# Attention of batch 0 in two query parts, with the first feed-forward matmuls beside the second part

## Chip, cores and metric

The kernel runs on one core of one Trainium2 chip. The metric is device time in microseconds (us) of that core. A "ratio" is the mean time of one kernel's runs over that of the other's runs of the same rounds, so it is not quite the ratio of the medians that are quoted.

Engines: PE is TensorE (matmul), ACT is ScalarE, DVE is VectorE, POOL is GpSimd, SP issues DMAs.

## The reference, cut to what matters

```python
# q, k, v: (8 batches, 12 heads, 448 tokens, 64); fp32
scores = q @ k.T / 8
attn   = maximum(scores, 0) ** 2 / 448
x      = (attn @ v), heads side by side          # 3584 tokens x 768
h      = maximum(x @ w_in, 0) ** 2               # w_in 768 x 2048
out    = h @ w_out                               # w_out 2048 x 768
```

## The kernel before

Heads go four at a time: a "unit" n is a third of a batch (24 units). A unit's score tile for key chunk t (64 keys) is 128 x 896; it is squared and masked on ACT and DVE ("soft"), and multiplied with v ("av"). The seven av steps of a unit sum into two PSUM tiles, which are copied to xt. When a batch's three units are done, its h groups (16 groups of 6 matmuls, each then squared into a tile g) and then its o groups (output) can run. Two stages follow from this. In the *stream*, batch 0's attention has nothing to hide behind. In the *dense stage*, PE works through a queue of h and o matmuls of one batch, and bursts of two score tiles of the next batch are put between them.

```python
def relu2(ps, dst, scale):                       # ACT Square, then DVE: (ps > 0) * dst
    nc.scalar.activation(out=dst, in_=ps, func=AF.Square, scale=scale)
    nc.vector.scalar_tensor_tensor(out=dst, in0=ps, scalar=0.0, in1=dst,
                                   op0=ALU.is_gt, op1=ALU.mult)
def relu2_wide(ps, dst, scale, eng):             # ACT Relu, then r*r on DVE or POOL
    ...
# the stream (batch 0 and two rounds of unit 3: 23 rounds)
for r in range(STREAM):
    n, t = divmod(r, TJ)
    sp = scores(n, t)                            # PE, 4 matmuls of 64x64 tiles, 448 columns
    soft(n, t, sp)                               # odd t: relu2_wide
    for z in late.get(r, (r - LAG,) if LAG <= r else ()):
        av(*divmod(z, TJ))                       # three rounds behind
    for fn, *a in beside.get(r, ()):             # casts, transposes, weight loads
        fn(*a)
push_dense(0)                                    # 16 h groups of 448 columns, then 6 o groups
for i in range(STREAM // 2, NB):                 # the dense stage
    ...                                          # two score tiles, av of a whole unit now and then
    run_some(max(0.0, (queued - KEEP) / (nxt - i)))
```

Score tiles live in two PSUM buffers (`sps`), everything else PE writes in four (`mmps`). PE, like SP, issues in the order in which the program is written. POOL issues the loads that change type (v and the weights), and casts q and k.

## Time and profile before

412.84 us (2 runs, 412.78 to 412.9); span 411.3 us.

| what | value | read from |
|---|---|---|
| stream, first score matmul to dense start | 7.84 to 37.86 us: 23 rounds, and the dense stage's first score tile at 37.34 us | timeline of PE |
| PE busy from 37.86 us to the end | 368.5 of 373.4 us; the rest is the last copy and store | table of stretches |
| PE waits in the stream | 9.7 us for score tiles to come free | waits |
| 128x896 eviction | ACT 0.92, DVE 1.09 us | groups |
| first 15 h matmuls | 5.24 us at half clock; later 3.00 us | timeline of PE |

The table of stretches of the kernel before (stretch in us, its length, then busy us and instructions of PE, PE's weight loads, DVE, ACT and POOL, then granted PE clock, DMA share and GB/s):

```profile
30.00:35.00 5.00, 2.74 (x32) 1.38 (x32) 4.14 (x4) 4.32 (x7) 0.74 (x1) 0.72 1.14 278
35.00:40.00 5.00, 4.32 (x26) 1.52 (x22) 3.61 (x5) 3.58 (x6) 0.67 (x1) 0.50 1.19 251
40.00:45.00 5.00, 5.00 (x36) 2.50 (x35) 2.81 (x5) 2.56 (x4) 1.19 (x3) 0.76 1.25 204
45.00:50.00 5.00, 5.00 (x33) 2.31 (x31) 4.69 (x7) 4.54 (x8) 4.61 (x7) 1.00 1.16 210
```

PE is full from 40 us on, but the clock is half until about 42 us. The whole dense stage in the same view:

```profile
37.86:411.27 373.41, 368.54 (x2860) 188.03 (x2856) 225.91 (x276) 233.72 (x376) 51.63 (x64) 0.99 0.55 116
```

The waits of the kernel before on PE, from 5 to 40 us (engine and line, for whom: us in total, times, longest):

```profile
PE sp L252 <- DVE at L155: 5.3, 4, 1.6
PE sp L252 <- ACT rel L161: 4.4, 4, 1.6
```

Both releasers free a score tile. No wait of PE is listed after the stream. The timeline of PE around the dense start (start us, us, instructions):

```profile
37.86 5.24 PE L176 MATMUL hps<-xt,w 128*128 128x448 f16 x15
...
44.33 3.00 PE L176 MATMUL hps<-xt,w 128*128 128x448 f16 x15
```

The same fifteen matmuls take 5.24 us, then 3.00 us.

### The profile page before, as it was taken

Reading aid. Unit: us, or ns where it says so; the run is one execution under the profiler, and the core shown is the slowest. Engines: PE = TensorE matmul, PEld = TensorE weight load, DVE = VectorE, ACT = ScalarE, POOL = GpSimd, SP = SyncE. Lnnn points to the kernel's source line nnn. Section 1 sums busy time; section 2 is a strip of 40 time slices with the busy share of each in tenths; the row PEclk is TensorE's granted clock in tenths of the full one; section 3 lists DMA queues with packets and bytes.
Section 4 is the critical chain, followed back from the end, with each engine's and each line's share of the span. In section 5 each row is a group of like instructions: output and inputs, shape, how many; then the busy total and the mean of one; then the engine's idle time right before and its main releaser. Section 6 shows DMA issues by size and latency. Waiting matters only on the chain.

```text
span 411.3 us, 7560 instructions
## 1 busy us (share of the span) xinstructions
PE 394.0 (96%) x3104; PEld 199.7 (49%) x3104; DVE 252.8 (61%) x304; ACT 259.7 (63%) x407; POOL 74.0 (18%) x95
## 2 busy tenths in 40 slices
PE   6847999999999999999999999999999999999995
PEld 2423455544455545544554544544554545555562
DVE  3987787578875777576655786576665686042200
ACT  3787787678866677666756767666756766333211
POOL 6861612123202301210302301210100000000000
PEclk9695999999999999999999999999999999999999
DMA  8999999599419750972829741881515010201132
GB/s 251 295 278 257 207 193 225 157 208 201 119 38 183 193 141 35 155 168 56 209 54 174 225 102 73 147 176 43 131 40 119 4 40 0 69 12 38 38 79 77
DMA packets 62914, 53.57 MB, mean 130 GB/s; under 512 B 35744, under 2 KB 59296, under 8 KB 62880
## 3 DMA queue, kind: packets, MB, share of 16 engines
q1 hardware_dynamic: 50672, 40.84, 40.7%
q0 software_dynamic: 11936, 11.80, 18.0%
q8 instruction: 24, 0.39, 0.4%
q10 hardware_dynamic: 272, 0.46, 0.3%
q14 instruction: 10, 0.08, 0.1%
HBM read 45.61 MB, written 11.01 MB: 138 GB/s over the span
## 4 chain that ended last, share of the span: by engine, by line
PE 91%; ACT 4%; DVE 2%; DMA 1%; issue 1%
PE hps L176 37%; PE ops L204 36%; PE sp L252 10%; PE avt L282 7%; ACT at L154 2%; ACT rel L161 1%; DMA kf<-in_k_dram 1%; DVE at L155 1%; PE tps L101 1%; ACT qT L103 0%; ACT xt L290 0%; DVE at L162 0%; DVE ks L87 0%; DVE kT L103 0%; DVE qT L103 0%
## 5 line engine op out<-in xcount | busy, mean ns | idle before, releaser
L155 DVE SCALAR_TENSOR_TENSOR at<-sp,at 128x896 f16<-128x896 f32 x159 | 166.3, 1085 | 82.1 <-ACT at L154 81.7
L154 ACT ACTIVATE at<-sp 128x896 f16<-128x896 f32 x159 | 137.7, 915 | 70.4 <-PE sp L252 70.4
L176 PE MATMUL hps<-xt,w 128*128 128x448 f16 x768 | 157.5, 356 | 0.0
L204 PE MATMUL ops<-w,g 128*128 128x384 f16 x896 | 156.8, 326 | 0.0
L204 PEld LDWEIGHTS <-g 128*128 128x128 f16 x896 | 84.4, 98 | 67.9 <-issue 13.7
L176 PEld LDWEIGHTS <-w 128*128 128x128 f16 x768 | 73.1, 99 | 75.1 <-issue 13.5
L155 DVE SCALAR_TENSOR_TENSOR g<-hps,g 128x448 f16<-128x448 f32 x128 | 75.7, 617 | 42.3 <-ACT g L154 42.0
L154 ACT ACTIVATE g<-hps 128x448 f16<-128x448 f32 x128 | 67.7, 551 | 29.7 <-PE hps L176 29.1
L252 PE MATMUL sp<-qT,kT 64*64 64x448 f16 x672 | 53.0, 373 | 10.6 <-DVE at L155 5.3
L211 ACT ACTIVATE osb<-ops 128x384 f32<-128x384 f32 x56 | 27.8, 496 | 37.8 <-PE ops L204 32.9
L87 POOL CAST ks<-kf 128x896 f16<-128x896 f32 x23 | 21.5, 935 | 147.6 <-DMA kf<-in_k_dram 109.8
L282 PE MATMUL avt<-at,vs 64*64 64x448 f16 x672 | 43.2, 363 | 0.4 <-ACT qT L103 0.3
L252 PEld LDWEIGHTS <-kT 64*64 64x64 f16 x672 | 16.5, 106 | 42.4 <-issue 39.7
L282 PEld LDWEIGHTS <-vs 64*64 64x64 f16 x672 | 21.5, 109 | 12.5 <-issue 2.7
L118 POOL DMA_DIRECT2D vs<-in_v_dram x28 | 17.4, 629 | 49.1 <-PE avt L282 48.3
L290 ACT ACTIVATE xt<-avt 128x448 f16<-128x448 f32 x48 | 23.6, 553 | 2.6 <-PE avt L282 2.5
L87 POOL CAST qs<-qf 128x896 f16<-128x896 f32 x23 | 23.2, 1009 | 6.7 <-DMA qf<-in_q_dram 6.7
L162 DVE TENSOR_TENSOR at<-rel 128x896 f16<-128x896 f32 x8 | 10.1, 1258 | 0.7 <-ACT rel L161 0.6
L161 ACT ACTIVATE rel<-sp 128x896 f32<-128x896 f32 x9 | 8.3, 922 | 2.2 <-PE sp L252 2.2
L345 PE MATMUL warm<-idle 128*128 128x512 f16 x12 | 4.6, 560 | 1.2 <-DVE idle L337 1.2
L129 POOL DMA_DIRECT2D w<-in_moe_w_out_dram x4 | 3.1, 764 | 14.2 <-DMA w<-in_moe_w_in_dram 14.2
L103 ACT COPY qT<-tps 128x896 f16<-128x896 f16 x5 | 4.5, 907 | 0.2 <-PE tps L101 0.2
(20 smaller groups left out, 31.4 us busy)
## 6 DMA issues: line engine op xcount, KB each, us to landing
kf<-in_k_dram SPq DMA_DIRECT2D x24, 448.0 KB, 5.1
out_dram<-osb SPq DMA_DIRECT2D x56, 192.0 KB, 2.7
qf<-in_q_dram SPq DMA_DIRECT2D x23, 448.0 KB, 5.7
vs<-in_v_dram POOLq DMA_DIRECT2D x28, 168.0 KB, 5.6
w<-in_moe_w_in_dram POOLq DMA_DIRECT2D x4, 768.0 KB, 22.2
w<-in_moe_w_out_dram POOLq DMA_DIRECT2D x4, 768.0 KB, 21.4
vs<-in_v_dram POOLq DMA_DIRECT2D x6, 112.0 KB, 7.9
qf<-in_q_dram ACTq DMA_DIRECT2D x1, 448.0 KB, 4.8
```

The costliest lines, as they stand in the source:

```text
L87: op(t.rearrange("p t (f d) -> p f t d", f=2), src.rearrange("p f (t d) -> p f t d", d=D))
L118: nc.gpsimd.dma_start(out=vst[b][rows, :, i], in_=src[:, :, h])
L154: nc.scalar.activation(out=dst, in_=ps, func=AF.Square, scale=scale)
L155: nc.vector.scalar_tensor_tensor(out=dst, in0=ps, scalar=0.0, in1=dst, op0=ALU.is_gt, op1=ALU.mult)
L161: nc.scalar.activation(out=r, in_=ps, func=AF.Relu, scale=scale)
L162: eng.tensor_mul(dst, r, r)
L176: nc.tensor.matmul(cell[0][:, 0:S], lhsT=w1[f // 4][:, m, (f % 4) * P:(f % 4 + 1) * P], rhs=xt[:, m, :], start=(m == 0), stop=(m == NM - 1))
L204: nc.tensor.matmul(cell[0][:, 0:HALF], lhsT=gt[f][:, tb * P:(tb + 1) * P], rhs=w2[f // 4][:, f % 4, hf * HALF:(hf + 1) * HALF], start=(f = ...
L211: nc.scalar.activation(out=cell[1][:, hf * HALF:(hf + 1) * HALF], in_=cell[0][:, 0:HALF], func=AF.Copy, scale=CO)
L252: nc.tensor.matmul(sp[64 * c:64 * c + 64, e, 0:S].rearrange("p (t c) -> p t c", t=TJ), lhsT=kT[r, t, 64 * e:64 * e + 64], rhs=qT[r, :, 64 ...
L282: nc.tensor.matmul(ap[f][64 * e:64 * e + 64, 0:S], lhsT=vs[r, u, e ^ c, t * D:(t + 1) * D], rhs=at[r, e, :], start=(t == 0), stop=(t == TJ ...
L290: nc.scalar.activation(out=xts[b][:, 2 * u + f, :], in_=ap[f][:, 0:S], func=AF.Copy, scale=CX)
```

## The change

The intent: batch 0's queries run as two parts, tokens 0 to 255, then 256 to 447. When the first part's attention is done, its columns of h can be computed beside the attention of the second part, where PE had idle time. Two key chunks share one score tile (2 x 256 = 512 or 2 x 192 = 384 columns). To have bandwidth for w_in in time, the loads of q and k for units 3 and 4 are put behind a "gate": a one-element memset in POOL's queue that the load must wait for. The first half of w_out's columns is loaded first. The diff, cut to its core:

```diff
-    def load_qk(n, w, eng):
+    def load_qk(n, w, eng, gate=None):
         ...
+        if gate is not None:
+            gate.memset(t[0:1, 0, 0:1], 0.0)
-    STREAM = NU * TJ + 2
+    STREAM = NU * TJ
+    PARTS = slice(0, 4 * TP), slice(4 * TP, S)
...
+        tiles = [(part, rounds[r:r + 2]) for part in range(2) for r in range(0, STREAM, 2)]
+        NA = len(tiles) // 2                                   # 11
+        engs = {1: nc.vector, 3: nc.vector, 5: nc.gpsimd, 7: nc.gpsimd, 9: nc.vector}
+        engs.update({NA + z: nc.gpsimd for z in (1, 3, 5, 7)})  # squares on POOL
+        engs[NA + 9] = nc.vector
         beside = {
...
+            NA + 1: [(load_w2, 0, 0), (load_w2, 0, 1),
+                     (load_qk, 3, "k", nc.sync, nc.gpsimd), (load_qk, 3, "q", nc.sync, nc.gpsimd)],
+            NA + 4: [(load_v, 1, slice(None))],
+            NA + 6: [(cast_qk, 3, "k", pool), (cast_qk, 3, "q", pool)],
+            NA + 7: [(load_qk, 4, "k", nc.sync, nc.gpsimd), (load_qk, 4, "q", nc.sync, nc.gpsimd)],
+            NA + 8: [(turn_pe, 3, "k", dve)],
+            NA + 9: [(turn_pe, 3, "q", act), (load_w2, 1, 0), (load_w2, 1, 1)],
         }
+        for i, (part, rs) in enumerate(tiles):
+            ...                                # scores of two chunks, soft
+            if i >= 2:
+                put(i - 2)                     # av, two tiles behind; part two's xt copies on DVE
+            if i > NA + 1:
+                for _, fn in h_group(0, done_h, PARTS[0]):
+                    fn()                       # one h group of 256 columns a tile, 11 in all
+                done_h += 1
...
-        hs = h_groups(b)
+        hs = h_groups(b) if b else (
+            [h_group(0, f, PARTS[0]) for f in range(done_h, NF)]
+            + [h_group(0, f, PARTS[1]) for f in range(NF)])
```

More of the change, by code (lines that the diff above doesn't have):

```diff
@@ L54 @@
     qkt_p = ctx.enter_context(tc.tile_pool(name="qktp", bufs=3))
-    at_p = ctx.enter_context(tc.tile_pool(name="atp", bufs=14))
+    at_p = ctx.enter_context(tc.tile_pool(name="atp", bufs=12))
     x_p = ctx.enter_context(tc.tile_pool(name="xp", bufs=2))
     g_p = ctx.enter_context(tc.tile_pool(name="gp", bufs=32))
-    rel_p = ctx.enter_context(tc.tile_pool(name="widep", bufs=5))
+    rel_p = ctx.enter_context(tc.tile_pool(name="widep", bufs=4))
     PSUM = bass.MemoryType.PSUM
@@ L120 @@
     w1 = [const_p.tile([P, NM, 512], FP16, name=f"w1_{i}", tag=f"w1_{i}") for i in range(4)]
-    w2 = [const_p.tile([P, 4, DM], FP16, name=f"w2_{i}", tag=f"w2_{i}") for i in range(4)]
+    w2 = [[const_p.tile([P, NF // 2, HALF], FP16, name=f"w2_{hf}{i}", tag=f"w2_{hf}{i}")
+           for i in range(2)] for hf in range(2)]
     def load_w1(i):
@@ L126, in load_w1, with load_w2 @@
             in_=moe_w_in[:, 512 * i:512 * (i + 1)].rearrange("(m p) f -> p m f", p=P))
-    def load_w2(i):
+    def load_w2(hf, i):
         nc.gpsimd.dma_start(
-            out=w2[i],
-            in_=moe_w_out[512 * i:512 * (i + 1), :].rearrange("(f p) d -> p f d", p=P))
+            out=w2[hf][i],
+            in_=moe_w_out[1024 * i:1024 * (i + 1), hf * HALF:(hf + 1) * HALF].rearrange(
+                "(f p) d -> p f d", p=P))
     fifo: deque = deque()
@@ L158, in relu2_wide, with h_group, step @@
     def relu2_wide(ps, dst, scale, eng):
-        r = rel_p.tile([P, 2, S], FP32, name="rel", tag="wide")
+        r = rel_p.tile([P, 2, 512], FP32, name="rel", tag="wide")
+        r = r[:, :, 0:ps.shape[-1]]
         nc.scalar.activation(out=r, in_=ps, func=AF.Relu, scale=scale)
         eng.tensor_mul(dst, r, r)
-    def h_groups(b):
+    def h_group(b, f, cols):
         pr = b // 2
-        if b % 2 == 0:
-            gts[pr] = [None] * NF
-        gt = gts[pr]
-        xt = xts[b]
+        gt = gts.setdefault(pr, [None] * NF)
         cell = [None]
-        def step(f, m):
+        w = cols.stop - cols.start
+        def step(m):
             def run():
@@ L176, in run, with h_groups, store @@
                 nc.tensor.matmul(
-                    cell[0][:, 0:S],
+                    cell[0][:, 0:w],
                     lhsT=w1[f // 4][:, m, (f % 4) * P:(f % 4 + 1) * P],
-                    rhs=xt[:, m, :], start=(m == 0), stop=(m == NM - 1))
+                    rhs=xts[b][:, m, cols], start=(m == 0), stop=(m == NM - 1))
                 if m == NM - 1:
-                    if b % 2 == 0:
+                    if gt[f] is None:
                         gt[f] = g_p.tile([P, 2 * S], FP16, name="g", tag="g")
-                    relu2(cell[0][:, 0:S], gt[f][:, (b % 2) * S:(b % 2 + 1) * S], 1.0)
-            return run
-        return [[(189.0, step(f, m)) for m in range(NM)] for f in range(NF)]
-    def store(pr, tb, osb):
+                    at = (b % 2) * S + cols.start
+                    relu2(cell[0][:, 0:w], gt[f][:, at:at + w], 1.0)
+            return run
+        return [(0.422 * w, step(m)) for m in range(NM)]
+    def h_groups(b):
+        return [h_group(b, f, slice(0, S)) for f in range(NF)]
+    def store(pr, tb, osb, cols):
         for i in range(2):
@@ L191, in store, with o_groups @@
             nc.sync.dma_start(
-                out=out[(2 * pr + b) * S:(2 * pr + b + 1) * S, :].rearrange(
+                out=out[(2 * pr + b) * S:(2 * pr + b + 1) * S, cols].rearrange(
                     "(p t) d -> p t d", t=TJ)[:, t, :],
-                in_=osb[64 * i:64 * i + 64, 0:DM])
-    def o_groups(pr, tb):
+                in_=osb[64 * i:64 * i + 64, 0:cols.stop - cols.start])
+    def o_groups(pr, tb, halves=False):
         gt = gts[pr]
@@ L205, in run @@
                     cell[0][:, 0:HALF], lhsT=gt[f][:, tb * P:(tb + 1) * P],
-                    rhs=w2[f // 4][:, f % 4, hf * HALF:(hf + 1) * HALF],
+                    rhs=w2[hf][f // 8][:, f % 8, :],
                     start=(f == 0), stop=(f == NF - 1))
                 if f == NF - 1:
-                    if hf == 0:
-                        cell[1] = rel_p.tile([P, 2 * S], FP32, name="osb", tag="wide")
+                    if hf == 0 or halves:
+                        cell[1] = rel_p.tile([P, 1024], FP32, name="osb", tag="wide")
+                    at = 0 if halves else hf * HALF
                     nc.scalar.activation(
-                        out=cell[1][:, hf * HALF:(hf + 1) * HALF],
+                        out=cell[1][:, at:at + HALF],
                         in_=cell[0][:, 0:HALF], func=AF.Copy, scale=CO)
-                    if hf == 1:
-                        store(pr, tb, cell[1])
+                    if halves:
+                        store(pr, tb, cell[1], slice(hf * HALF, (hf + 1) * HALF))
+                    elif hf == 1:
+                        store(pr, tb, cell[1], slice(0, DM))
             return run
@@ L232, in push_dense @@
             done = upto
-        new = [g for tb in (range(3) if b % 2 == 0 else range(3, 7)) for g in o_groups(b // 2, tb)]
+        if b == 0:
+            both = [o_groups(0, tb, halves=True) for tb in range(3)]
+            new = [both[tb][hf] for hf in range(2) for tb in range(3)]
+        else:
+            new = [g for tb in (range(3) if b % 2 == 0 else range(3, 7))
+                   for g in o_groups(b // 2, tb)]
         now = len(new) if b in (0, B - 1) else len(new) - 4
@@ L237, in push_dense, with scores @@
         carry = new[now:]
+    PARTS = slice(0, 4 * TP), slice(4 * TP, S)
+    WHOLE = slice(0, S)
     ats: dict = {}
-    def scores(n, t):
+    def scores(n, t, sp=None, at=0, cols=WHOLE):
         qT, kT = qkt[n, "q"], qkt[n, "k"]
-        sp = s_p.tile([P, 2, 512], FP32, name="sp", tag="s")
+        if sp is None:
+            sp = s_p.tile([P, 2, 512], FP32, name="sp", tag="s")
+        ts = slice(cols.start // TP, cols.stop // TP)
+        w = cols.stop - cols.start
         for e in range(2):
@@ L252, in scores, with soft, av @@
                 nc.tensor.matmul(
-                    sp[64 * c:64 * c + 64, e, 0:S].rearrange("p (t c) -> p t c", t=TJ),
+                    sp[64 * c:64 * c + 64, e, at:at + w].rearrange("p (t c) -> p t c", c=TP),
                     lhsT=kT[r, t, 64 * e:64 * e + 64],
-                    rhs=qT[r, :, 64 * e:64 * e + 64], start=True, stop=True)
-        return sp
-    def soft(n, t, sp):
-        at = at_p.tile([P, 2, S], FP16, name="at", tag="at")
-        if n < NU and t % 2 == 1:
-            relu2_wide(sp[:, :, 0:S], at, SK, nc.gpsimd if n == 1 and t == 3 else nc.vector)
-        else:
-            relu2(sp[:, :, 0:S], at, SK)
-        ats[n, t] = at
+                    rhs=qT[r, ts, 64 * e:64 * e + 64], start=True, stop=True,
+                    skip_group_check=True)
+        return sp
+    def soft(sp, width, eng=None):
+        at = at_p.tile([P, 2, 512], FP16, name="at", tag="at")
+        at = at[:, :, 0:width]
+        if eng is None:
+            relu2(sp[:, :, 0:width], at, SK)
+        else:
+            relu2_wide(sp[:, :, 0:width], at, SK, eng)
+        return at
     avs_open: dict = {}
-    def av(n, t):
+    def av(n, t, cols=WHOLE, copy=None):
         b, u = divmod(n, NU)
-        if n == NU * b and t == 0:
+        if b not in xts:
             xts[b] = x_p.tile([P, NM, S], FP16, name="xt", tag="xt")
+        w = cols.stop - cols.start
         vs = vst[b]
@@ L282, in av @@
                 nc.tensor.matmul(
-                    ap[f][64 * e:64 * e + 64, 0:S],
+                    ap[f][64 * e:64 * e + 64, 0:w],
                     lhsT=vs[r, u, e ^ c, t * D:(t + 1) * D],
@@ L289, in av @@
         for f in range(2):
-            nc.scalar.activation(
-                out=xts[b][:, 2 * u + f, :], in_=ap[f][:, 0:S], func=AF.Copy, scale=CX)
+            dst, src = xts[b][:, 2 * u + f, cols], ap[f][:, 0:w]
+            if copy is None:
+                nc.scalar.activation(out=dst, in_=src, func=AF.Copy, scale=CX)
+            else:
+                copy.tensor_scalar_mul(dst, src, CX)
     pool, dve, act = nc.gpsimd.tensor_copy, nc.vector.tensor_copy, nc.scalar.copy
@@ L309, in upkeep @@
     def upkeep(i):
+        if i == STREAM // 2:
+            for w in "kq":
+                cast_qk(4, w, pool)
+                load_qk(5, w, nc.sync)
         for n in range(NU, NUN):
             b, u = divmod(n, NU)
-            if i == max(TJ * n // 2, STREAM // 2):
+            if i == max(TJ * n // 2, STREAM // 2 + 2):
                 if 5 < n + 3 < NUN:
@@ L339 @@
         make_identity(nc, ident)
-        for u in range(NU):
-            load_v(0, u)
+        load_v(0, 0)
         warm = mm_p.tile([P, 512], FP32, name="warm", tag="mm")
@@ L349 @@
         turn_pe(0, "q", dve)
-        for w in "kq":
-            cast_qk(1, w, pool)
-        load_w1(0)
-        beside = {
-            1: [(load_w1, 1)],
-            2: [(cast_qk, 2, "k", pool), (cast_qk, 2, "q", pool),
-                (load_qk, 3, "k", nc.sync), (load_qk, 3, "q", nc.sync)],
-            3: [(turn_pe, 1, "k", dve), (load_w1, 2)],
-            5: [(turn_pe, 1, "q", act), (load_w1, 3)],
-            7: [(turn_pe, 2, "k", dve)],
-            8: [(turn_pe, 2, "q", act), (load_v, 1, slice(None))],
-            9: [(cast_qk, 3, "k", pool), (cast_qk, 3, "q", pool),
-                (load_qk, 4, "k", nc.sync), (load_qk, 4, "q", nc.sync)],
-            14: [(turn_pe, 3, "k", dve)],
-            15: [(turn_pe, 3, "q", act)],
-            16: [(cast_qk, 4, "k", pool), (cast_qk, 4, "q", pool),
-                 (load_qk, 5, "k", nc.sync), (load_qk, 5, "q", nc.sync)],
-            17: [(load_w2, 0), (load_w2, 1)],
-            19: [(load_w2, 2), (load_w2, 3)],
-        }
@@ L371 @@
-        late = {21: (18, 19), 22: (20,)}
-        for r in range(STREAM):
-            n, t = divmod(r, TJ)
-            sp = scores(n, t)
-            soft(n, t, sp)
-            for z in late.get(r, (r - LAG,) if LAG <= r else ()):
-                av(*divmod(z, TJ))
-            for fn, *a in beside.get(r, ()):
-                fn(*a)
+        cast_qk(1, "k", pool)
+        load_v(0, 1)
+        cast_qk(1, "q", pool)
+        load_v(0, 2)
+        cast_qk(2, "k", pool)
+        load_w1(0)
+        cast_qk(2, "q", pool)
@@ new lines @@
+        for i in (1, 2, 3):
+            load_w1(i)
+        rounds = [divmod(r, TJ) for r in range(STREAM)]
+        tiles = [(part, rounds[r:r + 2]) for part in range(2) for r in range(0, STREAM, 2)]
[3 more added lines that the diff above has]
+        engs[NA + 9] = nc.vector
+        beside = {
+            1: [(turn_pe, 1, "k", dve)],
+            2: [(turn_pe, 1, "q", act)],
+            4: [(turn_pe, 2, "k", dve)],
+            5: [(turn_pe, 2, "q", act)],
+            NA + 1: [(load_w2, 0, 0), (load_w2, 0, 1),
[5 more added lines that the diff above has]
+            NA + 9: [(turn_pe, 3, "q", act), (load_w2, 1, 0), (load_w2, 1, 1)],
+        }
@@ new lines, with put @@
+        done_h = 0
+        made: dict = {}
+        def put(i):
+            part, rs = tiles[i]
+            for n, t in rs:
+                ats[n, t] = made.pop((part, n, t))
+                av(n, t, PARTS[part], nc.vector if part else None)
+        for i, (part, rs) in enumerate(tiles):
+            cols = PARTS[part]
+            w = cols.stop - cols.start
+            sp = None
+            for j, (n, t) in enumerate(rs):
+                sp = scores(n, t, sp, j * w, cols)
+            at = soft(sp, len(rs) * w, engs.get(i))
+            for j, (n, t) in enumerate(rs):
+                made[part, n, t] = at[:, :, j * w:(j + 1) * w]
+            if i >= 2:
[4 more added lines that the diff above has]
+                done_h += 1
+            for fn, *a in beside.get(i, ()):
+                fn(*a)
@@ L380 @@
+        for i in (len(tiles) - 2, len(tiles) - 1):
+            put(i)
+            for _, fn in h_group(0, done_h, PARTS[0]):
+                fn()
+            done_h += 1
     tc.no_sync_barrier()
@@ L390 @@
                 av(avs[i], t)
-        for a in g:
-            soft(*a)
+        for n, t, sp in g:
+            ats[n, t] = soft(sp, S)
         if i in pushes:
```

## The prediction

> **What bounds it now.** By the table of time stretches PE is at 100% from 37.9 us to the end; the chain of waits gives PE 91% of the span. Before that, batch 0's attention streams 23 rounds between 7.8 and 37.9 us, 1.34 us a round. There PE waits to reuse score tiles, by the waits view for DVE L155 (5.3 us) and ACT L161 (4.4 us). By the timeline ACT works some 24 us of these 30, DVE 25. A 128x896 eviction takes ACT 0.92 us (0.82 start to start), DVE 1.09 (1.02). The granted clock is 0.5 from 11.7 to 18.5 us and from 32.2 to 42.4, so the first 15 h matmuls take 5.2 us against 2.9 later. DMA is saturated until 75 us; the four w1 loads land at 23.8, 31.3, 39.1 and 43.2 us.
>
> **What the change does.**
> - Queries of batch 0 run as 256 then 192 tokens, two key chunks to a tile: 11 + 11 tiles for 23 rounds. From 448 and 896 elements ACT costs about 0.19 us + 0.81 ns an element, so a 1024 tile needs about 1.02 us, DVE 1.22.
> - Eleven h groups of 256 columns (66 matmuls, about 108 ns from 190 ns per 448) run beside part two: 7.1 us leave the dense stage. This is the gain, all on the critical path.
> - PE works more in part two, so the clock should be full at the dense start: 2.3 us gained.
> - Two rounds of batch 1 go back to it: -0.4 us. 192-column h costs about 0.2 us more.
> - Six squarings go from DVE to POOL (1.68 us for 896 elements there), part two's six xt copies from ACT to DVE.
> - Without q/k 3 to 5 competing, w1 lands in time (estimated 18 to 34 us).
>
> **Does the stream lengthen?** Sums of start-to-start times: part one ACT 13.3, DVE 11 us; part two ACT 11.7, DVE 11.9, PE about 11 at full clock. In part one I take before's 81% of ACT: 16.4 us. In part two three engines are equally loaded and PE is in order, so I take 75%: 15.7 us. The stream ends near 39.8 us, 2 us later than before.
>
> **Given back after.** In the first dense stage the queue is shorter, so each burst of two score rounds has about 1.9 us of h instead of 2.8, but DVE still owes 2.0 us for the tiles and about 1.4 for g: DVE binds for about six bursts. I subtract 1 to 2 us.
>
> Sum: +7.1 +2.3 -0.6 -2 -1.3 = 5.5; I lean further down, as w2 comes in better order. Predicted 406.5 us, 80% range 402 to 410.5. Chances: faster by over 2% 0.33, within 2% 0.64, slower 0.03.
>
> **What would show it.** Stretch table: last part-two score tile at 36 to 41 us; h matmuls interleaved from about 26 us; clock 1.0 at the dense start; DVE over 90% and PE 85 to 95% in the next 12 us.
>
> **What would make it wrong.** A stream ending by 35 us (gain over 2%): larger tiles hide waits better than I take. POOL squarings on the chain. The Trainium skill ("GPSIMD Engine Reference", specification table) says POOL contends with DVE instructions with two SBUF inputs; this trace agrees: the DVE square took 1.07 us alone and 1.64 to 1.70 beside POOL casts. Late w2 halves, or a cold clock through part two (h at half rate), would undo it.

## The result and the profile after

425.41 us (2 runs, 425.39 to 425.43), ratio 1.0302 with a 95% interval of 1.0273 to 1.0332: slower. The span grew from 411.3 to 423.6 us.

The table of stretches of the changed kernel:

```profile
30.00:35.00 5.00, 4.30 (x82) 2.81 (x74) 2.91 (x7) 3.58 (x7) 5.00 (x9) 1.00 1.14 161
35.00:40.00 5.00, 3.60 (x62) 2.18 (x50) 2.87 (x5) 3.53 (x7) 2.18 (x3) 1.00 1.19 279
40.00:45.00 5.00, 0.88 (x19) 0.64 (x21) 2.87 (x6) 0.81 (x1) 3.72 (x6) 0.87 1.28 205
45.00:50.00 5.00, 5.00 (x47) 3.01 (x46) 0.98 (x2) 1.98 (x4) 2.32 (x3) 0.50 1.06 259
50.00:55.00 5.00, 5.00 (x52) 3.38 (x49) 3.44 (x8) 2.91 (x8) 3.92 (x7) 0.95 1.17 282
65.00:70.00 5.00, 2.82 (x33) 2.09 (x32) 4.10 (x9) 2.76 (x7) 0.00 (x0) 1.00 1.30 187
```

PE has 0.88 us of work between 40 and 45 us, then runs at half clock. It idles again later, at 65 to 70 us. The whole dense stage, from the end of the eleventh h group on:

```profile
51.98:423.60 371.62, 361.65 (x2899) 189.56 (x2898) 225.04 (x285) 232.99 (x381) 50.75 (x63) 1.00 0.51 113
```

The difference of 12.3 us is then a sum of four numbers (in us; "PE busy" from these stretches, idle time between the dense start and PE's last matmul):

| | before | after | difference |
|---|---|---|---|
| dense start | 37.86 | 51.98 | +14.1 |
| PE busy from there | 368.54 | 361.65 | -6.9 |
| PE idle from there | 0.0 | 5.0 | +5.0 |
| after the last matmul | 4.9 | 5.0 | +0.1 |

The two starts are not quite the same mark. After, the dense stage starts with its first score tile (51.98 us); before, 37.86 us is its first h matmul, and its first score tile came at 37.34 us. From tile to tile the start moves by 14.6 us and PE's busy time by -7.4 us (369.06 before). The text keeps 37.86 us, so what it calls "later than before" is about 0.5 us too small.

The chain of waits now has DVE at 6% and POOL at 1%, where before it had DVE 2% and no POOL:

```profile
PE 85%; DVE 6%; ACT 3%; DMA 2%; POOL 1%; issue 1%; SPq 0%; POOLq 0%
```

What happened between 38 and 52 us is seen in three views. PE's timeline (with the wait before an entry and who ended it in brackets):

```profile
38.40 0.83 PE L179 MATMUL hps<-xt,w 128*128 128x256 f16 x6
40.63 0.56 PE L103 MATMUL tps<-ident,ks 128*128 128x128 f16 x7 [1.40 <-POOL ks L89]
41.12 0.36 PE L274 MATMUL sp<-qT,kT 64*64 64x192 f16 x8
44.97 0.54 PE L307 MATMUL avt<-at,vs 64*64 64x192 f16 x8 [3.49 <-POOL qf L78]
45.44 1.46 PE L179 MATMUL hps<-xt,w 128*128 128x256 f16 x6
...
51.98 0.38 PE L274 MATMUL sp<-qT,kT 64*64 64x448 f16 x4
```

POOL's timeline:

```profile
28.08 1.47 POOL L167 TENSOR_TENSOR at<-rel 128x768 f16<-128x768 f32 x1 [4.64 <-ACT rel L166]
29.49 1.81 POOL L132 DMA_DIRECT2D w<-in_moe_w_out_dram  x2
31.28 0.09 POOL L78 MEMSET kf<- 1x1 f32 x1
...
35.36 1.48 POOL L167 TENSOR_TENSOR at<-rel 128x768 f16<-128x768 f32 x1
39.65 0.93 POOL L89 CAST ks<-kf 128x896 f16<-128x896 f32 x1 [2.81 <-DMA kf<-in_k_dram]
41.85 0.94 POOL L89 CAST qs<-qf 128x896 f16<-128x896 f32 x1 [1.28 <-DMA qf<-in_q_dram]
42.75 2.17 POOL L167 TENSOR_TENSOR at<-rel 128x768 f16<-128x768 f32 x1
44.86 0.09 POOL L78 MEMSET kf<- 1x1 f32 x1
```

And the DMA issues of the stretch 31.3 to 32 us (size, us from issue to landing):

```profile
kf<-in_k_dram SPq DMA_DIRECT2D x1, 448.0 KB, 8.1
qf<-in_q_dram SPq DMA_DIRECT2D x1, 448.0 KB, 9.9
```

The gate opened at 31.3 us, because POOL reached it only after a square and 1.8 us of issuing w_out loads. The k load then took 8.1 us and landed at about 39.5 us, the q load at 41.7. In the kernel before, unit 3's k load was issued at 5.95 us and landed at 15.2, 3.9 us before POOL's cast of it at 19.1 us. POOL waited for k with the cast at the head of its queue, and the square of the eighth tile of part two stood behind the two casts. ACT had finished that square's input at 37.1 us; it ran at 42.75. The Trainium skill ("TensorE: Matmul & The Clock Gate", Part 1) says that POOL's queue is strictly in order, and the trace agrees: POOL idled 2.8 us before 39.65, though this work was ready behind from 37.1 us on. PE, in order as well, waited 3.5 us for the product that needs the square. Note the name in brackets: the profile puts that wait down to the memset of the gate, "POOL qf L78", which is POOL's next instruction. By its end time and by what PE needed, the square at L167 is the releaser. An experiment below tests this.

The three longest waits of PE after 52 us in the changed kernel:

```profile
PE hps L179 <- DVE g L159: 2.6, 2, 1.3
PE sp L274 <- DVE at L159: 1.5, 3, 0.6
PE hps L179 <- DVE kT L105: 0.5, 1, 0.5
```

Before, there were none.

### The profile page after: what moved, and what is told of

Read it like the earlier page. It is cut to its first block, busy times and chain, and to the rows that moved or that the text cites. A ratio compares the mean times of both kernels' runs of the same rounds, so it can differ in the third digit from the quotient of the medians.

```text
span 423.6 us, 8146 instructions
## 1 busy us (share of the span) xinstructions
PE 398.9 (94%) x3368; PEld 212.5 (50%) x3368; DVE 251.2 (59%) x322; ACT 261.8 (62%) x424; POOL 82.8 (20%) x104
## 3 DMA queue, kind: packets, MB, share of 16 engines
q0 software_dynamic: 13984, 11.80, 18.4%
## 4 chain that ended last, share of the span: by engine, by line
PE 85%; DVE 6%; ACT 3%; DMA 2%; POOL 1%; issue 1%; SPq 0%; POOLq 0%
PE ops L211 34%; PE hps L179 32%; PE sp L274 9%; PE avt L307 7%; DVE at L159 4%; DMA qf<-in_q_dram 2%; ACT at L158 2%; PE warm L376 1%; ACT rel L166 1%; PE tps L103 1%; POOL at L167 1%; DVE at L167 1%; DVE kT L105 1%; DVE g L159 0%; POOL w L132 0%
## 5 line engine op out<-in xcount | busy, mean ns | idle before, releaser
L159 DVE SCALAR_TENSOR_TENSOR at<-sp,at 128x896 f16<-128x896 f32 (+2 forms) x159 | 165.7, 1081 | 89.1 <-ACT at L158 88.9
L158 ACT ACTIVATE at<-sp 128x896 f16<-128x896 f32 (+2 forms) x159 | 137.4, 910 | 70.8 <-PE sp L274 70.3
L179 PE MATMUL hps<-xt,w 128*128 128x448 f16 (+2 forms) x864 | 160.0, 335 | 3.3 <-DVE g L159 2.6
L159 DVE SCALAR_TENSOR_TENSOR g<-hps,g 128x448 f16<-128x448 f32 (+2 forms) x144 | 77.6, 567 | 48.2 <-ACT g L158 48.0
L158 ACT ACTIVATE g<-hps 128x448 f16<-128x448 f32 (+2 forms) x144 | 69.7, 510 | 36.7 <-PE hps L179 35.8
L274 PE MATMUL sp<-qT,kT 64*64 64x448 f16 (+2 forms) x756 | 54.4, 354 | 7.0 <-DVE at L159 2.5
L307 PE MATMUL avt<-at,vs 64*64 64x448 f16 (+2 forms) x756 | 43.6, 346 | 6.8 <-POOL qf L78 3.5
L317 ACT ACTIVATE xt<-avt 128x448 f16<-128x448 f32 (+1 forms) x48 | 22.6, 531 | 2.6 <-PE avt L307 2.5
L167 POOL TENSOR_TENSOR at<-rel 128x768 f16<-128x768 f32 (+1 forms) x6 | 10.4, 1729 | 7.1 <-ACT rel L166 7.1
L166 ACT ACTIVATE rel<-sp 128x1024 f32<-128x1024 f32 (+1 forms) x10 | 9.2, 920 | 4.0 <-PE sp L274 4.0
L167 DVE TENSOR_TENSOR at<-rel 128x1024 f16<-128x1024 f32 (+1 forms) x4 | 5.5, 1380 | 1.2 <-ACT rel L166 1.2
## 6 DMA issues: line engine op xcount, KB each, us to landing
w<-in_moe_w_out_dram POOLq DMA_DIRECT2D x4, 768.0 KB, 14.4
```

The costliest lines, as they stand in the source:

```text
L166: nc.scalar.activation(out=r, in_=ps, func=AF.Relu, scale=scale)
L167: eng.tensor_mul(dst, r, r)
L179: nc.tensor.matmul(cell[0][:, 0:w], lhsT=w1[f // 4][:, m, (f % 4) * P:(f % 4 + 1) * P], rhs=xts[b][:, m, cols], start=(m == 0), stop=(m == ...
L274: nc.tensor.matmul(sp[64 * c:64 * c + 64, e, at:at + w].rearrange("p (t c) -> p t c", c=TP), lhsT=kT[r, t, 64 * e:64 * e + 64], rhs=qT[r, ...
L307: nc.tensor.matmul(ap[f][64 * e:64 * e + 64, 0:w], lhsT=vs[r, u, e ^ c, t * D:(t + 1) * D], rhs=at[r, e, :], start=(t == 0), stop=(t == TJ ...
L317: nc.scalar.activation(out=dst, in_=src, func=AF.Copy, scale=CX)
```

## The experiments

All results are correct unless it is said otherwise. The medians of the kernel before in the four jobs were 412.84, 412.96, 413.07 and 412.99 us.

### First job: the late load, POOL's queue, the dense stage

Theory A: the late q/k load of unit 3 stalls part two. Rival B: part two is slow by itself, through POOL's squares and three evenly loaded engines.

**e1_gate3**: the load of unit 3 without the gate.

```diff
-                     (load_qk, 3, "k", nc.sync, nc.gpsimd), (load_qk, 3, "q", nc.sync, nc.gpsimd)],
+                     (load_qk, 3, "k", nc.sync), (load_qk, 3, "q", nc.sync)],
```

> The changed kernel with one edit: the loads of q and k of unit 3 no longer wait for a memset in POOL's queue, so they can be issued as soon as their buffers are free (about 6 us instead of 31.4). Theory A (the late q/k 3 load is what stalls part two: PE waits 1.4 us for the k transpose and 3.5 us for a square that stands in POOL's queue behind the casts, then runs at half clock from 43.7 to 50.5 us): both waits vanish, the clock is 1.0 at the dense start, the stream ends near 43 to 45 us instead of 52, the kernel takes 415 to 418 us. Rival B (POOL squares and three evenly loaded engines make part two slow whatever the loads do): under 3 us are gained, 422 to 424 us.

419.45 us, ratio 1.0159 (1.0141 to 1.0178). The timeline of PE in that run:

```profile
39.23 0.55 PE L103 MATMUL tps<-ident,ks 128*128 128x128 f16 x7
39.72 0.36 PE L274 MATMUL sp<-qT,kT 64*64 64x192 f16 x8
40.71 0.62 PE L307 MATMUL avt<-at,vs 64*64 64x192 f16 x8 [0.64 <-DVE xt L319]
...
45.81 0.38 PE L274 MATMUL sp<-qT,kT 64*64 64x448 f16 x4
```

Both waits are gone, the clock is full from 30.9 us on, and the dense stage starts at 45.81 instead of 51.98 us: 6.2 us. The time fell by 6.0 us, somewhat less than expected. Theory A is shown for these 6 us, but a start at 45.8 us is still 8 us later than in the kernel before, so B has a part.

**e3_w2later**: the gate stays; the first w_out loads are issued after the casts of unit 3.

```diff
-            NA + 1: [(load_w2, 0, 0), (load_w2, 0, 1),
-                     (load_qk, 3, "k", ...), (load_qk, 3, "q", ...)],
+            NA + 1: [(load_qk, 3, "k", ...), (load_qk, 3, "q", ...)],
-            NA + 6: [(cast_qk, 3, "k", pool), (cast_qk, 3, "q", pool)],
+            NA + 6: [(cast_qk, 3, "k", pool), (cast_qk, 3, "q", pool), (load_w2, 0, 0), (load_w2, 0, 1)],
```

> The changed kernel with the gate kept, but the first two w2 loads issued after the casts of unit 3 instead of just ahead of its gate. If the load is late because it shares the DMA queues with w2 and stands 1.8 us behind its issue on POOL, the q/k 3 landing moves from 39.5 and 41.7 us to about 34 and 36 us and most of the stall goes: 417 to 420 us. If it is late because the gate itself is placed too late (POOL reaches it only after the square of the second tile of part two, at about 29.5 us), less than 2 us are gained.

420.99 us. The loads were issued at 29.7 us and took 4.1 and 4.8 us: they landed at 33.9 and 35.0 us, as expected. So w_out's traffic and its issue together were what made the gated load land so late. The time is a little above the expected range, because the moved issues now stand between the casts and the eighth tile's square in POOL's queue: PE still waited 2.0 us there.

**e4_sq18**: only that square moves from POOL to DVE.

```diff
-        engs.update({NA + z: nc.gpsimd for z in (1, 3, 5, 7)})
+        engs.update({NA + z: nc.gpsimd for z in (1, 3, 5)})
+        engs[NA + 7] = nc.vector
```

> The changed kernel with the square of the eighth tile of part two moved from POOL to DVE, so that it no longer stands behind the late casts in POOL's queue. If the order of POOL's queue is what turns a late load into the 3.5 us wait of PE, that wait shrinks to about 1 us or less (DVE is free there), while the 1.4 us wait for the k transpose stays: 420 to 422 us. If the load alone matters, the wait moves to the q transpose and the time stays at 424 to 425 us.

420.69 us. The load is as late as before, and the wait for the k transpose stays, as PE's waits in that run have it:

```profile
PE tps L103 <- POOL ks L89: 2.1, 1, 2.1
```

But the 3.5 us wait is gone and the half clock after it lasts 3.4 us instead of 6.8. So the order of POOL's queue turned a late load into a long stall, and the wait that the profile names after the memset was a wait for the square.

**e5_sqdense**: in the first seven bursts of the dense stage, the second score tile is squared on POOL.

```diff
-        for n, t, sp in g:
-            ats[n, t] = soft(sp, S)
+        for j, (n, t, sp) in enumerate(g):
+            ats[n, t] = soft(sp, S, nc.gpsimd if j == 1 and i < 17 else None)
```

> The changed kernel, with the second score tile of each of the first seven bursts of the dense stage squared on POOL instead of DVE (ACT then does Relu instead of Square). If DVE binds that stage, as predicted, PE's idle time between 52 and 100 us (3.9 us up to 70 us and about 1 us later) falls to under 1.5 us and the kernel takes 421 to 423 us. If something else binds it (weights, clock, PSUM), the time stays within 1 us of 425.4.

421.84 us. The two longest waits of PE from its dense start on:

```profile
PE sp L274 <- DVE at L159: 1.2, 2, 0.6
PE hps L179 <- DVE g L159: 0.7, 2, 0.3
```

PE's idle time in the dense stage falls from 5.0 to 2.2 us, not quite to under 1.5; the rest of the gain is a start that came 0.7 us earlier in this run. DVE's work on score tiles does hold PE there. It is less a full DVE than an order: DVE was busy 10.2 of the first 12 us and less after that. It takes two score tiles (2.1 us) at once, the evictions of h stand behind them, and PE waits 1.3 us for one of its four PSUM buffers.

### Second job: both repairs, and what h beside part two is worth

**e6_both**: the edits of e1_gate3 and e5_sqdense together; the lines that they add are:

```diff
+                     (load_qk, 3, "k", nc.sync), (load_qk, 3, "q", nc.sync)],
+            ats[n, t] = soft(sp, S, nc.gpsimd if j == 1 and i < 17 else None)
```

> The changed kernel with both repairs: q/k 3 loaded early (gate removed) and the second tile of each of the first seven dense bursts squared on POOL. If the two losses are independent, their gains add (6.0 and 3.6 us of 425.4): 415 to 416.5 us, stream end near 46 us, PE idle between 46 and 70 us under 1 us. Still slower than before, because part two takes about 20 us at some 1.2 us of PE work a tile. If they overlap, 417 to 419 us.

416.6 us, ratio 1.0093 (1.0078 to 1.0108). The gains nearly add. This is 8.8 us better than the change and still slower than the kernel before. The dense stage starts at 46.49 us. A tile of part two at full clock, without a wait, in PE's timeline:

```profile
36.30 0.36 PE L274 MATMUL sp<-qT,kT 64*64 64x192 f16 x8
36.49 0.34 PE L307 MATMUL avt<-at,vs 64*64 64x192 f16 x8
36.76 0.83 PE L179 MATMUL hps<-xt,w 128*128 128x256 f16 x6
37.52 0.36 PE L274 MATMUL sp<-qT,kT 64*64 64x192 f16 x8
```

From score tile to score tile it takes 1.22 us. The matmuls alone should need 0.97 us, an estimate: six h matmuls at the median 109 ns from start to start, and 16 attention matmuls of 192 columns, four at a time, at 80 ns (192/448 of the 0.19 us that lie between one group of four of 448 columns and the next in PE's timeline of the kernel before, for example 24.33 and 24.52 us). Some 0.11 us goes at each change between 64x64 and 128x128 tiles (0.27 us from av to h less 0.16; 0.76 from h to scores less 0.65). The Trainium skill ("TensorEngine Tiling (Array Packing)", Key Properties) says that switching the tiling mode drains the engine; the trace agrees in that time is lost at both changes (0.11 us each), and shows nothing of what happens inside the engine.

All of part two in that run, in the table of stretches:

```profile
25.86:46.49 20.63, 18.41 (x268) 11.82 (x260) 13.04 (x25) 13.88 (x25) 13.69 (x16) 0.83 1.22 211
```

PE is busy 18.4 of these 20.6 us, at half clock until 32.7 us.

**e7_noh**: as e6_both, with no h group beside part two (the same lines after the loop, not shown, go too).

```diff
-            if i > NA + 1:
-                for _, fn in h_group(0, done_h, PARTS[0]):
-                    fn()
-                done_h += 1
```

> The kernel with both repairs, but no h group beside part two: all sixteen groups of 256 columns run in the dense stage. Theory A (h beside part two is paid for almost one to one, because PE is in order and already some 85% busy there): the stream ends 5 to 8 us earlier, near 38 to 41 us, and the total stays within 2 us of the kernel with both repairs. Rival B (the h work fills time in which PE would idle): the stream ends at most 3 us earlier and the total is 4 to 7 us longer.

422.66 us: 6.1 us slower than e6_both, though the stream ends 2.7 us earlier (43.76 against 46.49 us). Both are as rival B says, and theory A falls. The 6.1 us are a net figure and not a measure of the 7.1 us predicted for h alone. PE's busy time in the dense stage is 370.67 us here and 361.15 in e6_both. The difference of 9.5 us is near the 7.1 + 2.3 us that were predicted for h and the clock together: here the first 23 h matmuls of the dense stage took 4.53 us at half clock. The earlier end of the stream gives 2.7 us of it back. But even without any h, the stream ends 5.9 us later than in the kernel before, which does two rounds more by then. So it is not the h groups that cost. The rest of the change does: this kernel is 9.7 us slower than the kernel before, and the h groups earn 6.1 us of that back. What PE waits for in part two without h:

```profile
PE avt L307 <- POOL at L167: 4.9, 3, 2.5
PE avt L307 <- DVE at L159: 1.0, 1, 1.0
PE avt L307 <- POOL qf L78: 0.7, 1, 0.7
```

Mainly POOL, whose squares share its queue with casts and with the issue of the w_out and v loads.

**e8_fullh**: as e7_noh, with batch 0's h groups in full 448 columns.

```diff
-        hs = h_groups(b) if b else (...)
+        hs = h_groups(b)
```

> As the run without h beside part two, and the sixteen h groups of batch 0 in full 448 columns, not 256 and 192. If narrower h groups cost by their number (96 more matmuls, 16 more groups to evict on ACT and DVE), 0.5 to 2 us are gained over that run; if widths do not matter, the same time within 0.5 us.

420.56 us, 2.1 us less. PE's busy time in the dense stage falls by 1.06 us (370.67 to 369.61), its idle time from 1.0 to 0.1 us. Narrow groups cost by their number.

**e9_warm**: the kernel before, with eight idle matmuls after each av step, written with the start flag to unread columns of the av tile.

```diff
+                    for _ in range(FILL):       # FILL = 8
+                        nc.tensor.matmul(avs_open[z // TJ][0][:, 448:512], lhsT=idle[:, 0:P],
+                                         rhs=idle[:, 0:64], start=True, stop=True, ...)
```

> The kernel before, with eight idle matmuls of 64 columns after each attention-times-v step of the stream (into columns of the PSUM tile that nobody reads). If the half clock from 32.2 to 42.4 us comes from PE's idle time in the stream, the granted clock stays 1.0 from about 18 us, the first 15 h matmuls of the dense stage take about 2.9 us instead of 5.2 and the kernel gains 1.5 to 3 us: 410 to 411.5 us. If the fillers delay the score matmuls more than that, the stream ends later than 37.9 us and the time is 413 us or more.

411.75 us, ratio 0.9976 (0.9944 to 1.0007), and the **result was wrong** (relative error 0.26). The Trainium skill explains it ("PSUM — Partial Sum Buffer", The four PSUM rules, rule 2): a matmul with the start flag clears the accumulate bits of the whole bank in the quadrants it writes, so av's next matmul overwrote its sum. Fillers with `start=False` gave right results below. The clock was full at the dense start (38.98 us on), but the start came at 39.9 us, so there was no clear gain.

### Third job: POOL's queue without h, the clock, and edits of the kernel before

**e10_nohdve**: e7_noh with part two's four POOL squares on DVE.

```diff
-        engs.update({NA + z: nc.gpsimd for z in (1, 3, 5, 7)})
+        engs.update({NA + z: nc.vector for z in (1, 3, 5, 7)})
```

> The run without h beside part two, with the four POOL squares of part two moved to DVE. There PE waited 5.9 us for POOL squares, because POOL also issues w2 and v loads and casts. If POOL's queue is what makes part two 18 us long even without h, the stream ends near 39 us instead of 43.8 and the total falls from 422.7 to 418 to 419.5 us. If part two is long for other reasons (half clock, two-deep score tiles), the stream ends no earlier than 42.5 us.

420.2 us, 2.5 us less; the stream ends at 41.09 us. That is between the two expectations: taking the squares out of POOL's queue gives 2.7 us, and the two-part stream still ends 3.2 us later than the one of before. These 3.2 us hold several things at once (the division, the xt copies on DVE, the gate of unit 4, a clock of 0.5 through part two), and no run separates them.

**e11_fill**: e6_both with twelve idle matmuls (`start=False`, zeros) after most av steps of tiles 4 to 12.

```diff
+            if 3 <= i <= 12 and tiles[i - 2][1][-1][1] < TJ - 1:
+                for _ in range(12):
+                    nc.tensor.matmul(avs_open[...][0][:, 448:512], lhsT=idle[:, 0:P],
+                                     rhs=idle[:, 0:64], start=False, stop=False, ...)
```

> The kernel with both repairs, with twelve idle matmuls of 64 columns (zeros added into PSUM columns that nobody reads) after the attention-times-v step of most tiles from the fourth to the twelfth. If the half clock (12.2 to 32.7 us in that kernel) lengthens the stream, the clock is 1.0 for most of it, the three h groups that took 1.46 us each or waited behind cold tiles take 0.83, and the stream ends 2 to 3.5 us earlier: 413 to 415 us. If the fillers cost as much PE time as they give, 416 to 418 us.

415.85 us against 416.6: 0.2% less, at the edge of what the runs resolve (ratios 1.0074 and 1.0093, intervals that overlap). The clock was full from 16.5 us on. The table of stretches of e6_both:

```profile
25.00:40.00 15.00, 13.32 (x196) 8.66 (x196) 8.76 (x15) 10.77 (x19) 11.15 (x12) 0.74 1.23 192
```

and of e11_fill:

```profile
25.00:40.00 15.00, 12.39 (x233) 8.18 (x221) 9.04 (x15) 10.60 (x19) 11.66 (x12) 1.00 1.21 186
```

The clock of part two rose from 0.74 to 1.00, and the dense start moved only from 46.49 to 45.81 us. Waits took up much of the time: PE was idle 2.6 of these 15 us instead of 1.7, with 1.7 us of waits for POOL's squares from 25 us on. The fillers themselves took some 0.9 us of PE (two sets of twelve, 0.45 us each). The rival reading, that a cold clock is what holds the stream, is not borne out: less the price of the fillers, a full clock gave 0.7 us.

**e12_sqpool**: the kernel before, with the squares of its third unit on POOL. **e13_sqfill**: that, with twelve `start=False` fillers per av step from the fifteenth round on.

```diff
-            ... nc.gpsimd if n == 1 and t == 3 else nc.vector)
+            ... nc.gpsimd if n == 2 or (n == 1 and t == 3) else nc.vector)
```

The fillers of e13_sqfill:

```diff
+                if r >= 14 and z % TJ < TJ - 1:
+                    for _ in range(12):
+                        nc.tensor.matmul(avs_open[z // TJ][0][:, 448:512], lhsT=idle[:, 0:P],
+                                         rhs=idle[:, 0:64], start=False, stop=False, ...)
```

> The kernel before with one edit taken from the change: all three squares of the third unit of batch 0 go to POOL, which is nearly idle from 27 us on there. If DVE holds the score tiles in the last third of the stream, the dense stage starts 1 to 2 us earlier than 37.9 us and the time is 411 to 412 us; if ACT holds them, the same time within 0.5 us.

> The kernel before with the three POOL squares and twelve idle matmuls (zeros added into unread PSUM columns, so the result must be right this time) after each attention-times-v step from the fifteenth round on. If the clock of the dense start is worth 2.3 us and can be had for less than that, 409 to 411 us; if the fillers delay the score tiles, 412 us or more.

413.0 us (ratio 1.0011, 0.9986 to 1.0037) and 412.4 us (0.999, 0.9962 to 1.0017): no difference from the kernel before is shown. In e12_sqpool PE waited 1.6 us for a POOL square and the stream ended at 39.29 us, so the expected gain was not there.

### Fourth job: what still holds the stream

**e14_lag3**: e11_fill with av three tiles behind the scores. **e15_lag3act**: that, with part two's xt copies on ACT. **e16_lag3nofill**: e14_lag3 without the fillers.

```diff
-            if i >= 2:
-                put(i - 2)
+            if i >= 3:
+                put(i - 3)
...                                            # fillers and h groups one tile later, too
-                av(n, t, PARTS[part], nc.vector if part else None)
+                av(n, t, PARTS[part])                             # e15_lag3act alone
```

> The kernel with both repairs and the idle matmuls, with attention times v three tiles behind the score tiles instead of two. If PE's waits for POOL squares (2.7 us in all) and the other waits of those steps hold the stream, they nearly vanish and the stream ends near 43 us instead of 45.8: 413 to 414 us. If ACT and DVE hold it, the waits move to the score tiles and the stream ends at 45 to 46 us: 415.5 to 416.5 us.

> As the run with three tiles' lag, and the six xt copies of part two on ACT instead of DVE. If DVE's late xt copies (they hold PSUM tiles that the next unit's products need) cost PE's 0.6 us waits, another 0.5 to 1.5 us is gained; if ACT is the busier engine there, 0.5 to 1 us is lost.

> Three tiles' lag with both repairs, without the idle matmuls. If the clock matters once the waits for POOL are gone, it is 1 to 2.5 us slower than the run with them; if not, the same within 0.7 us.

417.27, 415.3 and 417.96 us. In e14_lag3 the waits for POOL disappeared and others came: from 25 us to the dense start 1.7 us for xt copies on DVE, 0.7 for one on ACT, 0.8 for g on DVE, and before that 1.8 us for DVE to free score tiles in part one. The dense stage started at 46.98 us, later than with two tiles' lag. So taking POOL's latency away moved the waits and did not shorten the stream; the h groups also start a tile later in this run. With the copies on ACT the start came at 45.08 us, and the two runs' intervals (1.0084 to 1.0126 and 1.0035 to 1.0075) do not overlap: a gain of about 2 us, above the range I gave. The fillers are not shown to matter (1.0105 against 1.012, overlapping). No version of the change that I tried beats the kernel before; e15_lag3act comes nearest, at 1.0055.

**e17_fill0**: the kernel before with the fillers of e13_sqfill alone (the second diff above for that pair, without the first).

> The kernel before with idle matmuls alone (twelve after each attention-times-v step from the fifteenth round on, zeros added). The run that also moved three squares to POOL had a full clock at the dense start, but PE waited 1.0 us for a POOL square and the stream ended 1.5 us late. Without that move: dense start near 38.5 us at full clock, 411 to 412 us, 0.3 to 0.5% faster than before. If the fillers themselves delay the stream, no gain.

412.24 us, ratio 0.9985 (0.9967 to 1.0003), not shown to be faster. Its dense start:

```profile
39.32 3.18 PE L176 MATMUL hps<-xt,w 128*128 128x448 f16 x15
```

The fifteen h matmuls take 3.18 instead of 5.24 us, but they start 1.5 us later: the fillers cost nearly what the clock gives. No kernel is shown to be faster than the kernel before.

## Why the prediction was wrong

Predicted: 406.5 us (402 to 410.5), most likely within 2%. Measured: 425.4 us, 3.0% slower.

1. **"The stream ends near 39.8 us, 2 us later than before": the step that failed.** It ended at 52.0 us, 14.1 us later. Of the 12.2 us by which the end was missed, 6.2 are the late load, 4.8 part two and 0.7 part one; the rest lies in the starts.
   - 6.2 us of this is the late q/k load of unit 3 (e1_gate3). The prediction asked whether w_in and w_out come in time. It did not ask when POOL would reach the gate that the diff adds, nor what stands behind a cast that waits.
   - Part one was about right: 16.4 us predicted, 17.1 measured (8.01 to 25.13 us).
   - Part two was put at 15.7 us, with PE's share at 11 us. Without the late load it took 20.5 us (25.35 to 45.81 in e1_gate3). PE alone needs about 14.4 us at full clock, an estimate from e6_both's timeline: 11 tiles of 1.22 us and two transposes of 0.5 us. The term was too small by 3.4 us. Some 2.4 us of this are 22 changes of tile mode at 0.11 us: 66 h matmuls at 108 ns and 42 groups of four attention matmuls at 80 ns make 10.5 us, so the 11 us had no room for them. The other 1 us is about what the transposes take. Had 14.4 us stood there, the prediction's own 75% would have given 19.2 us, so this term accounts for about 3.5 of the 4.8 us that part two was off.
   - What lies between 14.4 and 20.5 us is only in part idle time. In e6_both PE was busy 18.4 of 20.6 us. Its clock was half until 32.7 us, and at full clock the 6.3 busy us before that would be some 3 us less (an estimate that halves them). But e11_fill, with a full clock, started the dense stage only 0.7 us earlier: PE's busy time in part two fell to 16.75 us, and its idle time rose from 2.2 to 3.4 us. A longer lag gave nothing by itself; with that lag, taking part two's xt copies back from DVE to ACT gave 2 us (e15_lag3act), which was not tried with a lag of two tiles. So no single cause of this last part is shown.
2. **"7.1 us leave the dense stage": right in mechanism.** PE's busy time in the dense stage differs by 9.5 us between e7_noh and e6_both, for 7.1 + 2.3 predicted; that the whole time differs by 6.1 us, near 7.1, is chance, since this is a net of several terms. But the narrow groups cost 1.06 us of PE time (e7_noh against e8_fullh) where 0.2 was predicted. PE's busy time in the dense stage fell by 6.9 us; 8.8 had been predicted (7.1 + 2.3 - 0.6). Of the gap of 1.9 us, 0.9 is the narrow groups and 0.5 the mark at which the stage starts (see the sum above); about 0.5 us is not placed.
3. **"The clock should be full at the dense start: 2.3 us": right.** Fillers alone take 2.05 us off PE's dense time (368.54 to 366.49 in e17_fill0). In the changed kernel the half clock was paid inside the stream instead, from 43.7 to 50.5 us, after PE had stood idle. That it was full again 1.5 us before the dense start was luck there; without the late load (e1_gate3) it was full from 30.9 us on, as argued.
4. **"DVE binds for about six bursts; I subtract 1 to 2 us": right in kind, too small.** PE idled 5.0 us in the dense stage. In its first 12 us PE was 89% busy, in the range given, and DVE 85%, below the 90% given. From 64 to 72 us, later than I looked, PE worked only 5.4 of 8.0 us. Moving squares to POOL took 2.8 us of idle time away.
5. **What I named as a danger**: "POOL squarings on the chain" did come true, through the queue and not through their length. The POOL and DVE contention that I cited was there (a 128x1024 square on DVE took 1.54 and 1.60 us beside casts on POOL, 1.22 without), but it is tenths of a microsecond.

The sum on the measured side: 14.1 - 6.9 + 5.0 + 0.1 = 12.3 us.

## What to carry to other kernels

An in-order queue that both waits for loads and computes turns a late load into a stall of everything behind it; so when a change adds a gate, ask when that queue will reach it, and what stands behind the instruction that waits for it. Work moved into a stage's idle time is worth what it leaves behind, less what the stage must be cut into to make room for it: here the h groups earned 6.1 us, and all that came with the cut, both repairs made, had cost 9.7. When PE alternates between tile modes, count the changes as well as the columns, and read a tile's length from start to start in a trace.

## What the Trainium skill lacked or had wrong

- "TensorE: Matmul & The Clock Gate", Back-to-back issue gap: its formula of N/2.4 + 2.5 ns fits (109 ns for 256 columns, 83 for 192, 189 for 448). The page says that it over-counts at large N in a sustained stream, with about 131 ns for 512 columns; the sustained h matmuls of 448 columns here took 189 ns from start to start.
- The same page, Part 1, lets the clock fall after an idle window of about 3.4 us, and names micro-idles as a second case without a measure. Here the clock was halved at 32.2 us in the kernel before, although PE's longest idle time in the 3.4 us ahead of it was 1.6 us. The page does not say how busy is busy enough.
- "TensorEngine Tiling (Array Packing)", Key Properties, gives no figure for a change of tiling mode; about 0.11 us each is the estimate from e6_both's timeline.
